# Layer norm on ScalarE, FP32 head products from Q in PSUM, and a reordered front in a fused attention and gated-MLP kernel

## The chip, the cores and the metric

The kernel runs on one core of one Trainium2 chip. A core has five engines that each work through their own instruction queue in order: TensorE (PE, matrix products into PSUM), VectorE (DVE), ScalarE (ACT), GpSimd (POOL) and SyncE (SP, here only issuing DMAs). They meet through semaphores. The metric is the device time of one execution in microseconds. The kernel before took 272.57 us as the median of three runs (272.36 to 272.59).

## The reference

The input `x` has 2048 rows of 640. Two branches are added to it, both in bf16:

```
xn = layernorm(x)                                # no gain, no bias
q, k, v = split(xn @ wqkv)                       # 32 heads of 20
logits[h, s, w] = q[h, s] . k[h, s - 2w] / sqrt(20)      # w = 0..7, -1e9 where s - 2w < 0
A = (sum_w softmax_w(logits) * v[h, s - 2w]) @ wo
B = ((x2 @ w_gate) * (x2 @ w_up)) @ w_down       # x2 = xn
out = x + A + B
```

Each row attends to eight rows: itself and every second row behind it. So the logits are no matrix product. They are elementwise products of Q with eight shifted copies of K, each summed over the 20 channels of a head.

## The kernel before

The work stands channels-first: 640 channels are five chunks of 128 partitions, and the 2048 rows are four blocks of 512, called `j` here. The weight columns of Q and K are picked with a stride of five, so that a head's 20 channels lie as four neighbouring partitions in each of the five chunks.

- **Front** (`front`, L513 to L570). For each of 16 tiles of 128 rows: two `bn_stats` and one `bn_aggr` on DVE (L522, L525), a square root on ACT (L528), then a reciprocal and the normalisation on DVE (L532, L533). Tiles 0 to 4 are transposed by TensorE (L552) and copied by DVE (L560); the others by a transposing DMA (L567). Ahead of the first tile TensorE runs 22 products of zeros, and three more after the first transpose (`warm`, L572).
- **Projections** (`proj_qk`, `proj_v`, products at L590). Q and K are evacuated from PSUM by ACT (L595) into `QT` and `KT`, V into `VST` and then to a scratch tensor in HBM. The first two row tiles need only the Q weights, in two loads; the K weights come in the next load.
- **Products and head sums** (`products`, L715; `logits`, L733). For block `j`, each of the five chunks and each half `r` of the eight window places, DVE multiplies Q, repeated four times, with four shifted views of K: one bf16 instruction of 128 x 2048. There are 40, in twelve buffers `PRD`. TensorE sums over the channels with a 0/1 matrix `G`: four products of 32 columns for each buffer, 160 in all, accumulated over the five chunks.
- **Softmax** (L762 to L786) on DVE, exponential on ACT (L777), once for blocks 0 and 1, once for 2 and 3.
- **Weighted V** (`unit`). For each of 20 units (block, chunk) DVE multiplies the weights, held in PSUM, with shifted V (L879, FP32 results in `PV`), GpSimd adds pairs of those (L884), and TensorE sums over partitions (L925). The V views `VX` lie where `QT` and `KT` were.
- **Gated MLP and output** (`gu`, L966; `dn`, L1024). Gate and up products fill PSUM banks; ACT copies the gate half to `HT` (L595), DVE multiplies the up half into it (L975). `dn` accumulates twelve products with `WD` and five with `WO`, DVE adds x (L1035), and a DMA stores the tile.

**What sets the order.** `Sched.run` (L220) is a planner that runs when the program is built. Every step is a `Task` with an engine, a priority and what it reads; each operation has a cost in microseconds (`occ`). The planner takes the task that can start first on its own clocks, and lower priority numbers among those close by. The result is one fixed order for each engine, which the chip then follows: an engine whose next instruction waits does nothing else. `lock` makes the planner keep DVE and GpSimd operations that carry it apart in time.

`gu(0)` may begin when all Q and K are projected, `gu(1)` when V is and all four head sums are issued (L942 to L951), since `HT` lies over `WQKV` and over some `PRD`. Four more lines matter:

```
WQKV = sb("WQKV", [128, 3, NCH, D], at=a_ra)      # L377: Q, K, V in this order
K.spawn(proj_group([(which, m, 1)], j * JB, JB, 12 + j, None))      # L658: blocks 2 and 3
yield Task("pe", go, r=[slots[-1][1][:]], prio=9.5, banks=2, slack=0.5)      # L754: head sums
yield Task("pe", go, r=[SV[u % NS][:] for u in us], prio=9.7, banks=len(us), slack=0.7)      # L939
```

Of the kernel before, what the change touches and what calls it, by code (L numbers as in the profile page):

```python
# [9 lines left out]
D = 640  # L10
# [330 lines left out]
def build_kernel(nc, A_x, A_wqkv, A_wo, B_x, B_w_gate, B_w_up, B_w_down, out):  # L341
# [58 lines left out]
    ATX = [ATX0, sb("ATX1", [128, 2, 2, JB])]  # L400
    PRD += [sb("PRD10", [128, 4, JB], at=place[0] - 4096), sb("PRD11", [128, 4, JB], at=place[0])]
    NPR = len(PRD)
    NXR = 3
    a_xr = place[0]
    XR = sb("XR", [128, NXR, D])
# [4 lines left out]
    MV = sb("MV", [128, NT, 16], FP32)  # L410
    SD = sb("SD", [128, NT, 16], FP32)
    DUM = sb("DUM", [128, 16], FP32)
    ZERO = sb("ZERO", [128, JB])
    EPSC = sb("EPSC", [128, 16], FP32)
    IDENT = sb("IDENT", [128, 128])
# [5 lines left out]
    def ht(j, m):  # L421
        return HX[m][:] if j % 3 == 2 else HT[:, j % 3, m, :]

    done = set()
    count = {}

# [6 lines left out]
    def have(*k):  # L433
        return lambda: k in done

    def num(n, *k):
        return lambda: count.get(k, 0) >= n
# [32 lines left out]
    wqkv_src = A_wqkv.rearrange("(c p) n -> p c n", p=128)  # L470

    def wqkv_load(g, lo=0, hi=NCH):
        dst = WQKV[:, g, lo:hi, :]
        dma(dst, wqkv_src[:, lo:hi, g * D:(g + 1) * D], w=[dst], name=f"ld_wqkv{g}_{lo}")

    def loads():
# [36 lines left out]
    def front(t):  # L513
        x, st = XST[:, xslot(t), :], STATS[:, t, 0:12]
        xs, mv = XNS[:, t % NXN, :], MV[:, t, 0:2]
        sd, rstd = SD[:, t, 0:1], SD[:, t, 1:2]
        p = 0.1 * t

        def stats():
            for i in range(2):  # L520
                o, a = st[:, 6 * i:6 * i + 6], x[:, i * DHALF:(i + 1) * DHALF]
                op("dve", (lambda o, a: lambda e: e.bn_stats(o, a))(o, a), r=[a], w=[("st", t, i)], name=f"bn{t}_{i}", occ=0.49)  # L522

        def aggr():
            op("dve", lambda e: e.bn_aggr(mv, st), r=[("st", t, 0), ("st", t, 1)], w=[("mv", t)], name=f"bnag{t}", occ=0.2)  # L525

        def sqrt():
            op("act", lambda e: e.activation(sd, mv[:, 1:2], ACT.Sqrt, bias=EPSC[:, 0:1]), r=[("mv", t), EPSC[:]],  # L528
               w=[("sd", t)], name=f"sd{t}", occ=0.25)

        def apply():
            op("dve", lambda e: e.reciprocal(rstd, sd), r=[("sd", t)], w=[("rstd", t)], name=f"rstd{t}", occ=0.16)  # L532
            op("dve", lambda e: e.tensor_scalar(xs, x, mv[:, 0:1], rstd, op0=ALU.subtract, op1=ALU.mult),  # L533
               r=[x, ("mv", t), ("rstd", t)], w=[xs], name=f"lnap{t}", occ=0.45)
            mark("apply", t)

        yield have("x", t)
        yield Task("dve", stats, r=[x], prio=p)
        yield Task("dve", aggr, r=[("st", t, 1)], prio=p)
        yield Task("act", sqrt, r=[("mv", t)], prio=p)  # L540
        if t >= NXN:
            yield have("xnt", t - NXN)
        yield Task("dve", apply, r=[("sd", t), x], w=[xs], prio=p)
        o = XNT[:, :, t * TS:(t + 1) * TS]
        if t < N_PE_T:
            hold = []

            def trans(b):
                tpv = PS[:, b, :].bitcast(BF16)[:, 0:NCH * 128].rearrange("p (c f) -> p c f", c=NCH)
                for c in range(NCH):  # L550
                    i, q = xs[:, c * 128:(c + 1) * 128], tpv[:, c, :]
                    op("pe", (lambda q, i: lambda e: e.transpose(q, i, IDENT[:]))(q, i), r=[i, IDENT[:]], w=[q],  # L552
                       name=f"tr{t}_{c}", occ=0.057, lat=0.2)
                hold.append((b, tpv))
                if t == 0:
                    warm(3)

            def copy():
                b, tpv = hold[0]
                X = op("dve", lambda e: e.tensor_copy(o, tpv), r=[tpv], w=[o], name=f"xntcp{t}", occ=0.49)  # L560
                K.free_bank(b, X)

            yield Task("pe", trans, r=[xs], prio=p, banks=1)
            yield Task("dve", copy, r=[PS[:, hold[0][0], :]], prio=p)
        else:
            def dmat():
                op("sp", lambda e: e.dma_start_transpose(o, xs), r=[xs], w=[o], dma=True, name=f"dtr{t}", nbytes=200e3, occ=1.25, extra=1.3)  # L567

            yield Task("sp", dmat, r=[xs], prio=1)
        mark("xnt", t)  # L570
# [5 lines left out]

    def wcols(which, c, m):
        if which == 2:
            return WQKV[:, which, c, m * 128:(m + 1) * 128]
        return WQKV[:, which, c, m:D:NCH]  # L580

    def mms(parts, b, name):
        order = [(p, c) for p in parts for c in range(NCH)]
# [58 lines left out]
    def proj_qk():  # L642
# [11 lines left out]
        for j in (2, 3):  # L654
            yield have("xnt", 4 * j + 3)
            for m in range(NCH):
                for which in (0, 1):
                    K.spawn(proj_group([(which, m, 1)], j * JB, JB, 12 + j, None))  # L658

    def proj_v(j, m):  # L660
        hold = []
# [11 lines left out]
            yield have("xnt", t)  # L673
        for t in range(NT) if j >= 2 else range(8, 12) if j else ():
            yield have("apply", t)
        yield Task("pe", go, r=[WQKV[:, 2, 4, 0:64], XNT[:, NCH - 1, j * JB:(j + 1) * JB]], prio=30 + j, banks=1)
        yield Task("act", ev, r=[PS[:, hold[0], :]], prio=6)

    def store_v(j):
# [6 lines left out]

        yield Task("sp", go, r=[VST[:, j]], prio=20)

    pairs = [(j, r) for j in range(NJ) for r in (1, 0)]
    QORD = list(range(4))  # L690

    def products():
        n = 0
        for j, r in pairs:
            if r == 1:
                slots = []
            for c in range(NCH):
                for which in (0, 1):
                    yield num(4, "qk", which, j, c)
                    if which == 1 and j > 0:  # L700
                        yield num(4, "qk", 1, j - 1, c)
                if n % NPR == NPR - 1:
                    yield have("xnt", NT - 1)
                if n >= NPR:
                    yield have("prd", n - NPR)
                s = PRD[n % NPR]
                base = KT[:, c, :]
                lo = PAD + j * JB - DIL * (3 + 4 * (1 - r))
                kv = bass.AP(base.tensor, base.offset + lo, [base.ap[0], [DIL, 4], [1, JB]])
                q = QT[:, j, c, :]  # L710
                qb = q.unsqueeze(1).to_broadcast([128, 4, JB])
                rk = KT[:, c, lo:lo + JB + 3 * DIL]

                def go(s=s, kv=kv, q=q, qb=qb, rk=rk, c=c):
                    op("dve", lambda e: e.tensor_tensor(s[:], qb, kv, ALU.mult), r=[q, rk], w=[s[:]],  # L715
                       name=f"prod{j}_{r}_{c}", occ=1.15, lock=True)

                yield Task("dve", go, r=[q, rk], w=[s[:]], prio=20 + j, lock=True)
                slots.append((n, s, r, c))
                n += 1  # L720
            if r == 0:
                K.spawn(logits(j, slots))

    def logits(j, slots):
        hold = []

        def go(*bs):
            for n, s, r, c in slots:
                b = bs[1 - r]
                for a in range(4):  # L730
                    o = PS[32 * a:32 * a + 32, b, :].rearrange("p (q s) -> p q s", q=4)
                    x = s[:, :, a * TS:(a + 1) * TS]
                    op("pe", (lambda o, x, a, c: lambda e: e.matmul(o, G[:], x, start=(c == 0), stop=(c == NCH - 1),  # L733
                                                                   tile_position=(0, 32 * a)))(o, x, a, c),
                       r=[G[:], x], w=[o], name=f"lg{j}_{r}_{c}_{a}", occ=0.054, lat=0.4, mode=1)
                mark("prd", n)
            hold.extend(bs)

        def dst(r):
# [11 lines left out]
                        m = LOG[0][0:32, 0, 4 * r + s, 0:DIL * w]  # L751
                        op("pool", (lambda m: lambda e: e.memset(m, NEG))(m), w=[m], name=f"mask{w}", occ=0.2)  # L752

        yield Task("pe", go, r=[slots[-1][1][:]], prio=9.5, banks=2, slack=0.5)  # L754
        bump("lg")
        for r in (1, 0):
            yield Task("act", lambda: ev(r), r=[PS[:, hold[1 - r], :]], w=[dst(r)], prio=2)
# [183 lines left out]

    def gu(j):  # L942
        if j == 0:
            for which in (0, 1):
                for m in range(NCH):
                    for jj in range(NJ):
                        yield num(4, "qk", which, jj, m)
        elif j == 1:
            for jj in range(NJ):
                yield num(NCH, "v", jj)  # L950
            yield num(NJ, "lg")  # L951
        elif j == 2:
            yield have("atx", 1)
        else:
            yield num(8, "dn", j - 3)
        if j:
            yield have("gu", j - 1)
        for m in range(NF):
            h = ht(j, m)
            hold = []  # L960

            def go(which, b):
# [90 lines left out]
                K.spawn(fin_thread())  # L1053

    N_PE_T = 5
    FIRST = 9
    GU_KEEP = 3

    x_load(0)
    x_load(1)  # L1060
    wqkv_load(0, 0, 3)
    wqkv_load(0, 3, NCH)
# [1 line left out]
    wqkv_load(1)  # L1064
    x_load(3)
    K.t["act"] = 2.1
    warm(22)

    def misc():
        yield have("xnt", NT - 1)  # L1070

        def sel():
            for q in range(4):
                a, b = SEL[32 * q:32 * q + 32, :], IDENT[32 * q:32 * q + 32, 32 * q:32 * q + 32]
                op("dve", (lambda a, b: lambda e: e.tensor_copy(a, b))(a, b), r=[b], w=[a], name=f"sel{q}", occ=0.1)

        yield Task("dve", sel, prio=19)
        yield Task("act", lambda: op("act", lambda e: e.activation(DUM[:, 0:1], EPSC[:, 0:1], ACT.Exp), r=[EPSC[:]], w=[DUM[:]],
                                     name="exp_preload", occ=1.3), prio=6)
# [56 lines left out]
```

## Time and profile before

The profiled execution took 272.77 us, of which 270.8 us are its span from the first to the last instruction.

| | |
|---|---|
| median of three runs | 272.57 us |
| profiled execution, its span | 272.77 us, 270.8 us |
| DVE busy | 224.9 us (83%), 286 instructions |
| ACT busy | 93.2 us (34%), 169 instructions |
| POOL busy | 96.5 us (36%), 57 instructions |
| granted TensorE clock | 1.000 |
| all DMA | 33.46 MB, mean 124 GB/s |

Times are in microseconds from the start of the span. A row of a timeline gives start, duration, engine, line, operation, what is written and read, and how often; in brackets the idle time before it and who ended it. A row of the chain gives start, duration and what held the end of the program back at that time. A row of the groups gives all instructions of one line and shape: total busy time, mean of one in ns, then idle time before them. "Busy" of one instruction overlaps its neighbour when they follow closely, so the pace of a row of equal instructions is its total divided by their number.

### The profile page before, as it was taken

How to read it: one execution, taken by the hardware profiler on the slowest of the kernel's cores; microseconds unless marked ns; L12 is line 12 of the kernel's file. 1: busy time of each engine (PE TensorE's matmuls, PEld its weight loads, DVE VectorE, ACT ScalarE, POOL GpSimd, SP SyncE). 2: the span in 40 equal slices, each digit the busy share in tenths (PEclk: the TensorE clock that was granted, in tenths of full speed). 3: DMA queues.
4: the chain of work that ended last, by engine and by line, in shares of the span. 5: the costliest groups of instructions: out<-in, count | busy, mean ns of one | idle time of the engine just before them, and what ended most of it. 6: DMA issues, size and time to landing. Idle time of an engine off the chain costs nothing.

```text
span 270.8 us, 4489 instructions
## 1 busy us (share of the span) xinstructions
PE 265.4 (98%) x1811; PEld 153.6 (57%) x1811; DVE 224.9 (83%) x286; ACT 93.2 (34%) x169; POOL 96.5 (36%) x57
## 2 busy tenths in 40 slices
PE   7899999999999999999999999999999999999995
PEld 5897965454444444444444577544676776444775
DVE  5777799999999989999999999889989998623221
ACT  2466676555753245222433400433201202242000
POOL 1000000000000004077756876677857996600000
PEclk9999999999999999999999999999999999999999
DMA  6965459702343999127723356633364531100101
GB/s 202 361 207 83 92 81 322 264 0 97 99 130 78 240 207 319 39 49 163 177 69 80 105 130 166 185 83 79 79 174 132 138 88 48 48 2 0 48 27 48
DMA packets 39571, 33.46 MB, mean 124 GB/s; under 512 B 15232, under 2 KB 38272, under 8 KB 39552
## 3 DMA queue, kind: packets, MB, share of 16 engines
q1 hardware_dynamic: 39408, 33.15, 45.7%
q8 instruction: 14, 0.23, 0.4%
q10 hardware_dynamic: 144, 0.04, 0.1%
q14 instruction: 5, 0.04, 0.1%
HBM read 25.07 MB, written 5.26 MB: 112 GB/s over the span
## 4 chain that ended last, share of the span: by engine, by line
PE 89%; DVE 5%; DMA 3%; issue 1%; SPq 1%; ACT 0%; DVEq 0%
PE PS L966 33%; PE PS L1024 27%; PE PS L590 23%; DMA WQKV<-in_A_wqkv_dram 3%; PE PS L733 3%; PE PS L925 2%; DVE SM L762 2%; DVE PV L879 1%; SPq L446 1%; DVE HT L975 1%; DVE RS L782 1%; DVE M L762 0%; DVE LOG L773 0%; ACT PS L864 0%; PE PS L552 0%
## 5 line engine op out<-in xcount | busy, mean ns | idle before, releaser
L884 POOL TENSOR_TENSOR SV<-PV 128x1024 bf16<-128x1024 f32 x40 | 94.8, 2380 | 86.9 <-DVE PV L879 86.7
L879 DVE TENSOR_TENSOR PV<-VX,PS 128x1024 f32<-128x1024 bf16 (+1 forms) x56 | 92.9, 1670 | 1.7 <-ACT PS L864 1.7
L590 PE MATMUL PS<-XNT,WQKV 128*128 128x512 bf16 (+2 forms) x480 | 66.7, 299 | 1.2 <-DVE XNT L560 1.0
L966 PE MATMUL PS<-XNT,WG 128*128 128x512 bf16 x240 | 59.7, 379 | 0.1
L966 PE MATMUL PS<-XNT,WU 128*128 128x512 bf16 x240 | 59.7, 379 | 0.0
L590 PEld LDWEIGHTS PS<-XNT,WQKV 128*128 128x128 bf16 x480 | 43.4, 113 | 24.0 <-DVE XNT L560 1.7
L715 DVE TENSOR_TENSOR PRD<-QT,KT 128x2048 bf16<-128x2048 bf16 x40 | 46.1, 1218 | 0.0
L1024 PE MATMUL PS<-WD,HT 128*128 128x320 bf16 (+1 forms) x300 | 43.2, 294 | 0.0
L966 PEld LDWEIGHTS PS<-XNT,WU 128*128 128x128 bf16 x240 | 23.2, 98 | 29.1 <-ACT HT L595 0.8
L966 PEld LDWEIGHTS PS<-XNT,WG 128*128 128x128 bf16 x240 | 23.3, 98 | 28.6 <-DVE HT L975 0.6
L595 ACT ACTIVATE HT<-PS 128x512 bf16<-128x512 f32 x36 | 21.5, 597 | 51.6 <-PE PS L966 51.6
L1024 PEld LDWEIGHTS PS<-WD,HT 128*128 128x128 bf16 x300 | 28.6, 98 | 11.6 <-issue 0.4
L975 DVE TENSOR_TENSOR HT<-HT,PS 128x512 bf16<-128x512 bf16 x36 | 23.9, 683 | 12.7 <-PE PS L966 12.7
L1035 DVE TENSOR_TENSOR FOUT<-PS,XR 128x320 bf16<-128x320 f32 (+1 forms) x33 | 15.8, 478 | 16.9 <-PE PS L1024 16.5
L1024 PE MATMUL PS<-WO,OT 128*128 128x320 bf16 (+1 forms) x165 | 27.1, 295 | 0.0
L934 ACT ACTIVATE OT<-PS 128x512 bf16<-128x512 f32 x20 | 10.5, 600 | 36.8 <-PE PS L925 36.8
L1024 PEld LDWEIGHTS PS<-WO,OT 128*128 128x128 bf16 x165 | 15.9, 98 | 5.9
L752 POOL MEMSET LOG<- 32x6 bf16 (+6 forms) x7 | 0.4, 95 | 51.5 <-ACT LOG L744 51.5
L595 ACT ACTIVATE QT<-PS 128x512 bf16<-128x512 f32 (+1 forms) x22 | 12.3, 558 | 9.6 <-PE PS L590 9.5
L522 DVE BATCH_NORM_STATS2 STATS<-XST 128x6 f32<-128x320 bf16 x32 | 13.9, 476 | 2.0 <-DMA XST<-in_A_x_dram 1.9
L595 ACT ACTIVATE KT<-PS 128x512 bf16<-128x512 f32 (+1 forms) x22 | 12.2, 556 | 8.1 <-PE PS L590 8.1
L595 ACT ACTIVATE VST<-PS 128x512 bf16<-128x512 f32 x20 | 11.7, 597 | 8.1 <-PE PS L590 8.1
(43 smaller groups left out, 128.3 us busy)
## 6 DMA issues: line engine op xcount, KB each, us to landing
VX<-v_scratch SPq DMA_DIRECT2D x80, 130.0 KB, 2.9
XST<-in_A_x_dram SPq DMA_DIRECT2D x16, 160.0 KB, 7.1
v_scratch<-VST SPq DMA_DIRECT2D x4, 640.0 KB, 4.1
XR<-in_A_x_dram SPq DMA_DIRECT2D x16, 160.0 KB, 2.9
out_dram<-FOUT SPq DMA_DIRECT2D x15, 160.0 KB, 2.4
WG<-in_B_w_gate_dram SPq DMA_DIRECT2D x1, 1920.0 KB, 8.4
WU<-in_B_w_up_dram SPq DMA_DIRECT2D x1, 1920.0 KB, 12.0
WD<-in_B_w_down_dram SPq DMA_DIRECT2D x1, 1920.0 KB, 8.9
```

Of the source, the lines that this page charges most:

```text
L522: op("dve", (lambda o, a: lambda e: e.bn_stats(o, a))(o, a), r=[a], w=[("st", t, i)], name=f"bn{t}_{i}", occ=0.49)
L590: op("pe", (lambda o, l, x, c, first: lambda e: e.matmul(o, l, x, start=first, stop=(c == NCH - 1)))(o, l, x, c, first), r=[l, x], w=[o], ...
L595: X = op("act", (lambda o, i: lambda e: e.activation(o, i, ACT.Copy))(o, i), r=[i], w=[o], name=name, occ=0.12 + n * 0.9e-3)
L715: op("dve", lambda e: e.tensor_tensor(s[:], qb, kv, ALU.mult), r=[q, rk], w=[s[:]], name=f"prod{j}_{r}_{c}", occ=1.15, lock=True)
L733: op("pe", (lambda o, x, a, c: lambda e: e.matmul(o, G[:], x, start=(c == 0), stop=(c == NCH - 1), tile_position=(0, 32 * a)))(o, x, a, c) ...
L879: op("dve", lambda e: e.tensor_tensor(p, vw, a, ALU.mult), r=[vv] + rk, w=[p], name=f"pv{u}_{x}_{r0}", occ=0.09 + 1.1 * nr)
L884: X = op("pool", lambda e: e.tensor_tensor(o, p[:, :, 0, :], p[:, :, 1, :], ALU.add), r=[p[:]], w=[o], name=f"pva{u}_{x}", occ=2.36, lock= ...
L934: X = op("act", (lambda o, b: lambda e: e.activation(o, PS[:, b, :], ACT.Copy))(o, b), r=[PS[:, b, :]], w=[o], name=f"oev{u}", occ=0.58)
L966: op("pe", (lambda l, x, c: lambda e: e.matmul(PS[:, b, :], l, x, start=(c == 0), stop=(c == NCH - 1)))(l, x, c), r=[l, x], w=[PS[:, b, :] ...
L975: X = op("dve", lambda e: e.tensor_tensor(h, h, PS[:, hold[1], :], ALU.mult), r=[h, PS[:, hold[1], :]], w=[h], name=f"h{m}_{j}", occ=0.65)
L1024: op("pe", (lambda l, x, i: lambda e: e.matmul(dst, l, x, start=(i == 0), stop=(i == n - 1)))(l, x, i), r=[l, x], w=[PS[:, b, :]], name=f" ...
L1035: X = op("dve", lambda e: e.tensor_tensor(o, PS[:, b, 0:wid], xr, ALU.add), r=[PS[:, b, :], xr], w=[o], name=f"fin{t}_{nb}", occ=0.15 + wi ...
```

## The change

Six things are changed together.

1. **Normalisation.** For tiles 6 to 15 the normalisation is one ACT instruction, `Identity(x * rstd + nmr)`, with both scalars read per partition. DVE makes `nmr = -mean * rstd` with one more small instruction. The reciprocal is a task of its own, the two `bn_stats` are separate tasks, and the square root gets a better priority.
2. **Block 3.** For chunks 0 to 3 Q is not evacuated. Its bank is kept, and DVE multiplies it, from PSUM, with two shifted views of K at a time into an FP32 buffer of 128 x 1024 (`PRD32`, which lies over `PRD`): 16 instructions in place of 8. GpSimd adds the results of chunks 0 and 1, and of 2 and 3, into bf16 buffers: 8 additions. The head sums of block 3 take 6 buffers and 24 products instead of 10 and 40.
3. **Buffers.** `PRD` slots come from a free list instead of a ring.
4. **Weights.** In SBUF the order is now K, V, Q. `gu(0)` waits for K and V, `gu(1)` for Q, and the head-sum condition moves to its seventh group.
5. **Start.** 18 products of zeros instead of 22; the first statistics of tile 1 follow the ones of tile 0 at once.
6. **A small DMA** on ACT's queue reads 128 pieces of 64 bytes of `wqkv` into an unused buffer.

The core of the diff:

```diff
@@ front @@
-    sd, rstd = SD[:, t, 0:1], SD[:, t, 1:2]
+    sd, rstd, nmr = SD[:, t, 0:1], SD[:, t, 1:2], SD[:, t, 2:3]
...
+    def recip():
+        op("dve", lambda e: e.reciprocal(rstd, sd), r=[("sd", t)], w=[("rstd", t)], name=f"rstd{t}", occ=0.16)
+        if t >= N_DVE_A:
+            op("dve", lambda e: e.tensor_scalar(nmr, mv[:, 0:1], rstd, -1.0, op0=ALU.mult, op1=ALU.mult),
+               r=[("mv", t), ("rstd", t)], w=[("nmr", t)], name=f"nmr{t}", occ=0.13)
...
+            op("act", lambda e: e.activation(xs, x, ACT.Identity, bias=nmr, scale=rstd),
+               r=[x, ("nmr", t), ("rstd", t)], w=[xs], name=f"lnap{t}", occ=0.75)
...
-    yield Task("dve", stats, r=[x], prio=p)
+    if t == 1:
+        yield have("sd", 0)
+    for i in range(2):
+        yield Task("dve", lambda: stats(i), r=[x], prio=-1 if t == 1 and i == 0 else p)
     yield Task("dve", aggr, r=[("st", t, 1)], prio=p)
-    yield Task("act", sqrt, r=[("mv", t)], prio=p)
+    yield Task("act", sqrt, r=[("mv", t)], prio=p - 1)
+    yield Task("dve", recip, r=[("sd", t)], prio=p)
@@ proj_qk @@
-                    K.spawn(proj_group([(which, m, 1)], j * JB, JB, 12 + j, None))
+                    if which or j not in WIDE or m == NCH - 1:
+                        K.spawn(proj_group([(which, m, 1)], j * JB, JB, 12 + j, None))
@@ products @@
+def q_bank(j, c, hold):
...
+    yield Task("pe", go, r=[wcols(0, NCH - 1, c), XNT[:, NCH - 1, j * JB:(j + 1) * JB]], prio=8, banks=1, keep=1)
+def wide(j, slots):
+    for c0 in (0, 2):
...
+        for r in (1, 0):
...
+            for q0 in (0, 2):
+                for c in (c0, c0 + 1):
...
+                    def go(o=o, qb=qb, kv=kv, q=q, rk=rk):
+                        X = op("dve", lambda e: e.tensor_tensor(o[:], qb, kv, ALU.mult), r=[q, rk], w=[o[:]],
+                               name=f"prow{j}_{r}_{c}_{q0}", occ=1.17)
...
+                K.spawn(pair_add(j, s, n, q0, f, parts))
+def pair_add(j, s, n, q0, f, parts):
...
+        op("pool", lambda e: e.tensor_tensor(o, a[:], b[:], ALU.add), r=[a[:], b[:]], w=[o], name=f"padd{j}_{n}_{q0}",
+           occ=2.36, lock=True)
@@ gu @@
     if j == 0:
...
+                yield num(4, "qk", 1, jj, m)
         for jj in range(NJ):
             yield num(NCH, "v", jj)
-        yield num(NJ, "lg")
+    elif j == 1:
...
+                yield num(4, "qk", 0, jj, m)
...
+        if j == 1 and m == 6:
+            yield num(NJ, "lg")
@@ start @@
+N_DVE_A = 6
 x_load(0)
+tch = A_wqkv.rearrange("(p r) n -> p r n", r=NCH)[:, 0, 0:32]
+stores.append(dma(TCH[:], tch, w=[TCH[:]], name="touch", eng="act"))
 x_load(1)
...
-warm(22)
+warm(18)
```

In the fixed orders that the planner now writes, TensorE has the same 160, 120 and 200 projection products of 128, 256 and 512 columns. Five of 256 columns (the last chunk of Q for tiles 0 and 1) stand ahead of the first K group instead of behind it. The first head sums stand 20 products of 512 columns earlier. The head sums of block 3 stand behind 125 products from those of block 2 on, instead of 55: twelve gate and up pairs are done by then. At the end, the sums of the last two units stand behind all of `gu(3)`, directly ahead of `dn(3)`.

## The prediction

> **What bounds the kernel now.** I read the busy shares first, then the chain that ended last, then TensorE's rows at the start, then the groups by shape.
>
> ```profile
> PE 265.4 (98%) x1811; PEld 153.6 (57%) x1811; DVE 224.9 (83%) x286; ACT 93.2 (34%) x169; POOL 96.5 (36%) x57
> ```
>
> TensorE is busy for 98% of the span. The chain shows the same, and where its work stands:
>
> ```profile
> 3.24 7.55 DMA WQKV<-in_A_wqkv_dram
> ...
> 10.84 3.55 PE PS L590 x60
> 14.38 0.28 PE PS L552 x5
> 14.66 0.55 PE PS L590 x5
> ...
> 16.84 34.21 PE PS L590 x245
> 51.05 2.27 PE PS L733 x40
> ...
> 249.51 18.53 PE PS L1024 x153
> ```
>
> The end is set by the K weights, which land at 10.79, and from then on by TensorE's own work. The table of stretches has TensorE busy for 5.96 of 6.00 us from 10.84, all of 16.84 to 96.0, and all but some 0.1 us up to 230. So only two things shorten this kernel: less TensorE work behind 10.84, or more of it ahead of that point. Anything done on DVE, ACT or POOL pays only by not making TensorE wait.
>
> The start, from TensorE's timeline:
>
> ```profile
> 1.26 4.59 PE L574 MATMUL PS<-ZERO 128*128 128x256 bf16 x22 [1.26 <-DVE EPSC L449]
> 9.03 1.31 PE L590 MATMUL PS<-XNT,WQKV 128*128 128x128 bf16 x20 [0.72 <-DVE XNT L560]
> 10.18 0.44 PE L552 MATMUL PS<-IDENT,XNS 128*128 128x128 bf16 x5
> 10.84 3.55 PE L590 MATMUL PS<-XNT,WQKV 128*128 128x128 bf16 x60 [0.22 <-DMA WQKV<-in_A_wqkv_dram]
> ```
>
> There is a hole of 0.72 us before Q of tile 1 and one of 0.22 before K: about one microsecond in which Q work could stand. The durations that I use, from the groups by shape:
>
> ```profile
> L879 DVE TENSOR_TENSOR PV<-VX,PS 128x1024 f32<-128x1024 bf16 x32 | 38.2, 1213 | 1.7 <-ACT PS L864 1.7
> L715 DVE TENSOR_TENSOR PRD<-QT,KT 128x2048 bf16<-128x2048 bf16 x40 | 46.1, 1218 | 0.0
> L884 POOL TENSOR_TENSOR SV<-PV 128x1024 bf16<-128x1024 f32 x40 | 94.8, 2380 | 86.9 <-DVE PV L879 86.7
> L528 ACT ACTIVATE SD<-MV,EPSC 128x1 f32<-128x1 f32 x16 | 4.6, 290 | 5.3 <-DVE MV L525 5.2
> L1078 ACT ACTIVATE DUM<-EPSC 128x1 f32<-128x1 f32 x1 | 0.2, 203 | 0.0
> ```
>
> **Less TensorE work.** The head sums of block 3 fall from 40 products to 24. Forty take 2.27 us on the chain, 0.057 each; 16 of them are 0.91 us, and they stand where TensorE is never idle. All other counts of products are equal in both orders. That is the first term: **-0.91**.
>
> **More ahead of the K weights.** Five products of 256 columns (last chunk of Q, tiles 0 and 1) move from behind the first K group to before it; the chain gives them 0.55 us at 14.66. Is there room? Four zero products fewer (22 took 4.43 us up to the transpose at 5.69, 0.20 each) end the fill at about 4.9 to 5.1. Statistics of tile 1 go into the gap of the first square root, so the normalisation of tile 0 ends near 5.4 instead of 5.26 and the transpose starts there, not at 5.69. Q of tile 0 then starts near 6.45 (was 6.72). For tile 1, its copy is queued behind one `bn_stats` instead of two (0.44 us less than 8.50, with the wait for the transpose about 8.25), and Q runs from 8.75 to 10.06. The moved five end at 10.61, the transpose of tile 2 (0.28) at 10.89. K can start at 10.89 against 10.84. Net **-0.50**. I let the K weights land as before: the small new DMA has 128 pieces, and the nearest row, queue q10, spent 0.1% of sixteen engines' span on 144 packets, 0.27 us for each DMA engine. So it costs 0 to 0.3, where the hole leaves about 0.05; it could also make the weights earlier, but then DVE holds TensorE at 10.89 all the same. Its issue on ACT (about 0.4 us, as SP's) lies ahead of the table load, and the first square root starts only at 4.28.
>
> The Trainium skill speaks against cutting the fill. TensorE: Matmul & The Clock Gate, Part 1, says that TensorE starts at half clock and needs some 3.4 us of sustained work, measured in a free-running window, to be let up. The granted clock column shows 1.00 throughout, but the rows agree with the page: the zero products took 0.20 us each, while 256 columns later take 0.11. The change happened before 5.69, near 5.4 if the first twenty took 0.213. With 18 the fill would end at 5.1 and leave a gap of 0.3 us right there. By the rows the clock rises as before and the term stays -0.50; by the rule a missed window would leave it low until about 8.8, everything up to Q of tile 1 starts 0.5 us later, and the term is 0. I take the rows, as nine tenths of the window stay busy, and keep +0.5 for the range.
>
> **ACT in the front.** The row for 512 elements (0.597) and for 256 (0.383) give 0.84 ns an element, so 0.71 us for 640 without scalar operands. The skill, ScalarE: Activation LUTs, What ACT_TABLE_LOAD costs, says that each per-partition operand adds about 93 ns; the rows say 87 (290 with one, 203 without). With two, 0.89 to 0.92; I take 0.92, of which the next instruction overlaps 0.09. The loop from one tile to the next: normalisation 0.83, square root 0.29, reciprocal and new scalar 0.16 each with 0.04 hand-over: 1.56 to 1.6 us. ACT's queue agrees, 0.83 + 0.2 + one evacuation at 0.5 back to back. With 0.71 it would be 1.4. Before, tile 6 was normalised at 20.38 and tile 15 at 38.07, 1.97 us a tile. So with 1.58 tile 15's scalars stand at 20.4 + 9 x 1.58 = 34.6.
>
> Who waits for that? Evacuations are queued behind the normalisations: four or five are late at once near 33 us, of eight banks. Then the products. The first is done by 34.9, tile 15's two scalars (0.4), a second product, four small copies (0.7), eight more products at 1.14 (26.21 us for 23): the tenth ends near **46.2**. The first head sums stand 20 products of 0.216 earlier, and TensorE reaches them at 51.05 - 4.32 - 0.50 = **46.2**. Before, DVE was ready 1.6 us ahead. This is a tie; I charge **+0.1**, and keep 0 to 1.0.
>
> **Block 3.** Sixteen FP32 products are near the PV row (same shape, a PSUM operand, FP32 out): 1.21 busy, 1.14 at pace, 18.2 us, for eight at 9.1. They run between 76.7 and 101 with ten multiplications of the up half (0.60 each), while TensorE has gate and up work until about 107; the last two bf16 products end near 105.6, so 1.5 us spare. Eight GpSimd additions, 2.36 each, lie beside that. PV products beside additions show no slowing. Two-input SBUF work does: `SM` at 105.63 took 3.18 us for two where the earlier pair took 1.15, beside an addition that took 3.26. That price, 2.0 once, stands in both kernels; a second time, at the last bf16 products, it would overdraw the 1.5 by 0.5.
>
> **Weighted V comes later.** Softmax of blocks 2 and 3 ends near 122.3 instead of 111.8. Counting DVE's order at pace (2.2 for a PV of 2048, 0.60, 0.41 for an output), unit 2 ends near 138.2, its addition near 140.7; TensorE arrives near 141.4. Before, the addition ended at 130.2 and TensorE came at 130.97: the same 0.7 to 0.8 us. Unit 19 ends near 243.4 with the idle time of before (7 us), its addition at 245.8, TensorE at 247.4. No wait, so **0**; bounds 0 to 0.8. It cannot gain, as TensorE was not waiting there. Four evacuations fewer, the free list and the weights' order likewise: nothing waited for them. The price if that cover goes is in the rivals.
>
> **Sum.** -0.91 - 0.50 + 0.10 = -1.31 us. The profiled execution would take 272.77 - 1.31 = 271.46; it lies 0.20 above the median, so the median goes to 272.57 - 1.31 = **271.3**.
>
> **Rivals.**
> - *The gain is partly eaten at the start* (the clock comes up late, K lands late, or the first head sums wait 0.3 to 1.0): for it, the tie at 46.2 and a hole of 0.05; against it, that the tie comes from DVE's measured pace. Gain 0.56 to 1.0, **271.8**.
> - *The start gives nothing and DVE is late somewhere behind it*, at unit 2 or at block 3, whose slacks are 0.7 and 1.5: gain 0.91 less some 0.8, **272.5**, no difference.
> - *ScalarE becomes the bound of the front, and it gets slower.* Place: the loop from tile 6 to 15. Every 0.1 us more on a tile makes the tenth product 0.9 us later, and TensorE stands before the first head sums with nothing else in its order. Above 1.58 + 1.4/9 = 1.74 us a tile the whole gain is gone; if each tile also waits for a full evacuation (0.3 more, 1.88), the wait is 2.7 us and the time **273.9**. For it: ACT stands in this loop twice and its queue has an evacuation for each tile. Against it: these evacuations are ready before their turn by my times.
>
> **How the numbers follow.** A difference of 0.2%, 0.55 us, is about what a measurement of this kernel can tell from none. The forecast has 0.56, the eaten gain 0.25, no difference 0.10, slower 0.09. Faster 0.81, the same 0.10, slower 0.09. The range: no wait and K at 10.84 give 271.1, with DVE or the weights better than I count some 0.3 less; the upper end takes in the eaten gain and the edge of no difference: 270.8 to 272.3.
>
> **What would show it.** 144 head sums on TensorE, busy about 264.5; the 60 K products start near 10.9 with 45 Q products ahead of them; no idle before the first head sums near 46.2 (a wait for DVE `PRD` there is the second or fourth case, and its length says which); the normalisation near 0.92 on ACT and 1.6 us from tile to tile; FP32 products near 1.21; DVE busy near 232, POOL 115, ACT 100; head sums of block 3 near 107. I am wrong if TensorE shows waits of over 0.3 us before any head sum, or if its idle time ahead of 10.9 is not filled.

## The result, and the profile after

The changed kernel took 271.47 us, the median of six runs (271.11 to 272.07), beside 272.47 us for the kernel before on the same chip (six runs, 272.08 to 272.59). The ratio is 0.9967, with a 95% interval of 0.9954 to 0.998: about 0.9 us faster. The profiled execution also took 271.47 us, with a span of 269.7 us. By the chain, TensorE's last product ended at 267.01 instead of 268.04, which is 1.03 us earlier. The granted clock of the run was 1.000.

The busy shares on the page of the changed kernel:

```profile
PE 264.3 (98%) x1791; PEld 152.7 (57%) x1791; DVE 231.9 (86%) x294; ACT 98.4 (36%) x175; POOL 115.2 (43%) x65
```

TensorE has 20 instructions fewer: 16 head sums and four products of zeros. DVE has 7 us more and GpSimd 19 us more, and TensorE is still the engine that sets the time. Here is its chain, with start, duration and what held the end back:

```profile
10.99 3.35 PE PS L610 x60
...
16.80 29.35 PE PS L610 x220
46.15 2.27 PE PS L816 x40
...
107.27 1.41 PE PS L816 x24
108.68 13.05 PE PS L1052 x60
121.73 0.08 issue
121.81 0.02 DVEq L319
121.83 0.79 issue
122.62 0.69 DVE HT L1061
123.32 0.04 issue
123.36 18.52 PE PS L1052 x85
141.88 0.76 PE PS L1008 x12
...
248.37 18.64 PE PS L1110 x153
```

Three things are to be seen. The first head sums (x40) follow their predecessor without any pause. The head sums of block 3 are 24 products in 1.41 us. And at 121.7 the chain leaves TensorE for 1.6 us: it goes over issue time (in which an engine waited for nothing that the profile shows) to a multiplication of DVE (L1061, the up half into `HT`), and only then on with gate and up products at 123.36. The kernel before had such a place too, among the lines of its chain that the prediction left out: from 96.0 to 112.5 its chain runs over the softmax on DVE, and it comes back to TensorE here:

```profile
111.78 0.69 DVE HT L975
...
112.52 18.52 PE PS L966 x85
```

TensorE's timeline at the start. The last column, in brackets, is the idle time ahead and who ended it:

```profile
1.26 4.02 PE L594 MATMUL PS<-ZERO 128*128 128x256 bf16 x18 [1.26 <-DVE EPSC L453]
5.38 0.71 PE L569 MATMUL PS<-IDENT,XNS 128*128 128x128 bf16 x5
...
8.86 1.86 PE L610 MATMUL PS<-XNT,WQKV 128*128 128x128 bf16 x25 [0.58 <-DVE XNT L578]
...
10.83 3.51 PE L610 MATMUL PS<-XNT,WQKV 128*128 128x128 bf16 x60
```

Ahead of the K group (x60) stand 25 Q products in a row where 20 stood before. The hole ahead of K is gone, and that ahead of Q of tile 1 is 0.58 instead of 0.72. Three groups by shape (line, total, mean ns, idle time before):

```profile
L780 DVE TENSOR_TENSOR PRF<-PS,KT 128x1024 f32<-128x1024 f32 x16 | 19.0, 1218 | 0.3 <-PE PS L816 0.2
...
L546 ACT ACTIVATE XNS<-XST,SD 128x640 bf16<-128x640 bf16 x10 | 9.2, 920 | 0.9 <-DVE SD L538 0.9
L816 PE MATMUL PS<-PRD,G 128*32 128x512 bf16 x144 | 8.5, 380 | 0.0
```

### Where the time went

One number makes the runs comparable. The start of the K group shifts from run to run by some tenths (it stands at 10.6 to 11.4 in the traces below). What follows it does not: the stretch from the start of the K group to TensorE's last product repeats to 0.01 us in kernels that are equal behind that point. The start is read from the timeline, the end from the chain. The chain can't be used for the start: where a group follows another without a wait, the chain begins it at the end of the one before, here 0.16 us late (10.99 where the timeline has 10.83), and where TensorE waited, at its own start. In this table, "hole" is what TensorE loses behind the softmax of blocks 2 and 3: the start of the first late group of five gate or up products, less the time it was due, 1.08 us after the group before it began. (The idle time in a bracket is 0.16 less, as the profile lets each group end 1.24 us after its start.)

| kernel | K starts | first head sums | end of TensorE | K to end | hole |
|---|---|---|---|---|---|
| before | 10.84 | 51.05 | 268.04 | 257.20 | 0.30 |
| after | 10.83 | 46.15 | 267.01 | 256.18 | 0.71 |
| e1 | 10.87 | 46.19 | 269.40 | 258.53 | 2.18 |
| e2 | 11.29 | 52.00 | 274.30 | 263.01 | 0.70 |
| e3 | 10.82 | 46.68 | 267.53 | 256.71 | 0.70 |
| e4 | 11.16 | 46.49 | 266.63 | 255.47 | none |
| e5 | 10.70 | 47.12 | 267.96 | 257.26 | 0.70 |
| e6 | 10.93 | 51.64 | 267.54 | 256.61 | 0.29 |
| e7 | 10.90 | 46.25 | 267.27 | 256.37 | none |
| e8 | 10.92 | 46.24 | 267.10 | 256.18 | 0.70 |
| e9 | 11.36 | 46.68 | 266.82 | 255.46 | none |
| e10 | 10.63 | 45.95 | 266.09 | 255.46 | none |
| e11 | 11.06 | 48.54 | 270.40 | 259.34 | 0.70 |
| e12 | 10.91 | 51.12 | 267.81 | 256.90 | none |

The hole in the kernel before, from the timelines of TensorE and of DVE over 100 to 118 us:

```profile
111.14 1.24 PE L966 MATMUL PS<-XNT,WU 128*128 128x512 bf16 x5
112.52 1.25 PE L966 MATMUL PS<-XNT,WG 128*128 128x512 bf16 x5
```

```profile
110.64 1.22 DVE L786 TENSOR_TENSOR LOG<-LOG,RS 128x2048 bf16<-128x2048 bf16 x1
111.78 3.07 DVE L975 TENSOR_TENSOR HT<-HT,PS 128x512 bf16<-128x512 bf16 x5
```

Groups of five follow each other by 1.08 us, so the one at 112.52 was due at 112.22. The multiplications that empty its PSUM banks were queued behind the last step of the softmax and began at 111.78. In the changed kernel the same thing is larger (timeline of all engines, 104 to 127 us):

```profile
115.22 1.22 DVE L845 TENSOR_TENSOR SM<-LOG 128x1024 f32<-128x1024 bf16 x1
115.38 3.27 POOL L967 TENSOR_TENSOR SV<-PV 128x1024 bf16<-128x1024 f32 x1 [11.69 <-DVE PV L962]
...
116.47 3.19 DVE L845 TENSOR_TENSOR SM<-SM 128x512 f32<-128x512 f32 x2
...
119.69 1.75 DVE L865 RECIPROCAL RS<-SM 128x256 bf16<-128x256 f32 x1
...
121.48 1.22 DVE L869 TENSOR_TENSOR LOG<-LOG,RS 128x2048 bf16<-128x2048 bf16 x1
...
122.62 2.47 DVE L1061 TENSOR_TENSOR HT<-HT,PS 128x512 bf16<-128x512 bf16 x4
...
123.36 1.25 PE L1052 MATMUL PS<-XNT,WU 128*128 128x512 bf16 x5 [0.55 <-DVE HT L1061]
```

From 115.2 to 122.6 DVE works through the softmax in one piece. Four multiplications of the up half wait behind it, each holding a bank. TensorE runs out of free banks; the group due at 122.65 starts at 123.36. That is 0.71 us lost where 0.30 was lost before. DVE's rows of this stretch are the same in both kernels, 10.84 us later now (111.78 and 122.62), while the group of TensorE was due only 10.43 us later (112.22 and 122.65): TensorE comes 0.41 us earlier to the same wait.

So the 1.03 us come out of the trace in three terms. The first head sums were due at 51.05 - 20 x 0.216 = 46.73 if nothing had changed but the order of the projections, and started at 46.15: **-0.58** for the start. Forty head sums take 2.27 us and 24 take 1.41: **-0.86**. The hole: 0.71 - 0.30 = **+0.41**. The sum is -1.03.

### The profile page after: what moved, and what is told of

It is laid out like the page before. It is cut to its first block, busy times and chain, and to the rows that moved or that the text cites. A ratio compares the mean times of both kernels' runs of the same rounds, so it can differ in the third digit from the quotient of the medians.

```text
span 269.7 us, 4474 instructions
## 1 busy us (share of the span) xinstructions
PE 264.3 (98%) x1791; PEld 152.7 (57%) x1791; DVE 231.9 (86%) x294; ACT 98.4 (36%) x175; POOL 115.2 (43%) x65
## 4 chain that ended last, share of the span: by engine, by line
PE 96%; DVE 2%; DMA 1%; issue 0%; DVEq 0%
PE PS L1052 38%; PE PS L1110 28%; PE PS L610 24%; PE PS L816 3%; PE PS L1008 2%; DMA XST<-in_A_x_dram 1%; PE PS L569 1%; DVE STATS L525 0%; DVE XNT L578 0%; DVE HT L1061 0%; DVE XNS L543 0%; DVE FOUT L1121 0%; DVE MV L528 0%; DVE SD L536 0%; DVEq L319 0%
## 5 line engine op out<-in xcount | busy, mean ns | idle before, releaser
L738 DVE TENSOR_TENSOR PRD<-QT,KT 128x2048 bf16<-128x2048 bf16 x32 | 36.8, 1218 | 0.0
L794 POOL TENSOR_TENSOR PRD<-PRF,PRF 128x1024 bf16<-128x1024 f32 x8 | 18.8, 2357 | 35.5 <-DVE PRF L780 35.5
L1061 DVE TENSOR_TENSOR HT<-HT,PS 128x512 bf16<-128x512 bf16 x36 | 24.1, 682 | 6.8 <-PE PS L1052 5.6
L780 DVE TENSOR_TENSOR PRF<-PS,KT 128x1024 f32<-128x1024 f32 x16 | 19.0, 1218 | 0.3 <-PE PS L816 0.2
L525 DVE BATCH_NORM_STATS2 STATS<-XST 128x6 f32<-128x320 bf16 x32 | 14.7, 469 | 2.0 <-DMA XST<-in_A_x_dram 2.0
L947 ACT ACTIVATE PS<-ATX 128x512 f32<-128x512 bf16 x8 | 4.8, 598 | 27.4 <-DVE PV L962 27.4
```

The source lines that it names most:

```text
L525: op("dve", lambda e: e.bn_stats(o, a), r=[a], w=[("st", t, i)], name=f"bn{t}_{i}", occ=0.49)
L780: X = op("dve", lambda e: e.tensor_tensor(o[:], qb, kv, ALU.mult), r=[q, rk], w=[o[:]], name=f"prow{j}_{r}_{c}_{q0}", occ=1.17)
L794: op("pool", lambda e: e.tensor_tensor(o, a[:], b[:], ALU.add), r=[a[:], b[:]], w=[o], name=f"padd{j}_{n}_{q0}", occ=2.36, lock=True)
L1061: X = op("dve", lambda e: e.tensor_tensor(h, h, PS[:, hold[1], :], ALU.mult), r=[h, PS[:, hold[1], :]], w=[h], name=f"h{m}_{j}", occ=0.65)
```

## The experiments

My theory after the result: start and head sums are worth what they should be, and the difference is lost in the hole, because DVE's order puts the up multiplications behind the softmax. The rivals: the start is worth nothing; ScalarE is at its limit; the parts can be had singly. Times are medians; each ratio is to the kernel before on the same chip.

### e1: without the FP32 products

```diff
-    WIDE = (3,)
+    WIDE = ()
```

> The changed kernel with block 3 as before (WIDE empty: Q of block 3 is evacuated, ten bf16 products, 40 head sums); normalisation on ScalarE and the new start stay. Theory (the gain is TensorE's own work: 0.91 us of head sums, about 0.5 us moved ahead of K, less 0.4 us more of a wait for PSUM banks behind the second softmax): 0.91 comes back, of the wait 0.4 goes, so about 0.5 us slower than the changed kernel, 272.0. Rival (the normalisation on ScalarE is what pays, by relieving VectorE): no difference, 271.5.

Measured: 273.46 us (273.09 to 274.43), ratio 1.0042, interval 1.0026 to 1.0059. Slower than the kernel before, so both expectations missed. TensorE's timeline and DVE's, around 108 us:

```profile
109.56 1.25 PE L1052 MATMUL PS<-XNT,WG 128*128 128x512 bf16 x5 [2.01 <-DVE HT L1061]
```

```profile
108.83 3.07 DVE L1061 TENSOR_TENSOR HT<-HT,PS 128x512 bf16<-128x512 bf16 x5
```

The hole is 2.18 us (idle 2.01). With DVE less loaded, the softmax of blocks 2 and 3 begins earlier (96.45), and five multiplications pile up behind it. Beside the kernel before, the start is worth -0.59 here (as in e6, from K to the end) and the hole +1.88, together +1.29; "K to end" is 1.33 longer. So the hole depends on where the planner puts the softmax among the multiplications. It made e1 useless as a price of the head sums; e7 is the repair.

### e2: the normalisation on DVE

```diff
-    N_DVE_A = 6
+    N_DVE_A = NT
```

> The changed kernel with all 16 normalisations on VectorE again (N_DVE_A = 16); block 3 and the start stay. Theory: VectorE is later by about 3.5 us in the front, the planner puts gate and up groups or projections ahead of the first head sums instead, and TensorE does the same work without waiting: 271.5, within 0.2 us of the changed kernel. Rival (the normalisation is what pays): back to the kernel before, 272.5.

Measured: 278.52 us (278.02 to 278.79), ratio 1.0223 (1.0209 to 1.0238): both missed by six us. TensorE's timeline at 162 us, and its stretches of 2 us (busy times of the five engines, then the granted clock, then the share and rate of the DMAs):

```profile
165.99 0.39 PE L1008 MATMUL PS<-SV,SEL 128*32 128x512 bf16 x2 [2.83 <-POOL SV L967]
168.30 0.61 PE L1008 MATMUL PS<-SV,SEL 128*32 128x512 bf16 x2 [1.92 <-POOL SV L967]
168.84 3.11 PE L1110 MATMUL PS<-WD,HT 128*128 128x320 bf16 x12
...
172.47 1.79 PE L1110 MATMUL PS<-WD,HT 128*128 128x320 bf16 x12
```

```profile
167.00:169.00 2.00, 0.70 (x3) 0.23 (x4) 2.00 (x2) 0.04 (x1) 2.00 (x2) 0.78 0.75 186
169.00:171.00 2.00, 2.00 (x9) 1.10 (x8) 2.00 (x2) 0.55 (x1) 2.00 (x2) 0.50 0.15 29
```

TensorE waits 2.83 and 1.92 us for GpSimd's additions before the second sums over partitions (L1008). The reason lies 100 us earlier: with the slow loop of the front and the 9 us of extra FP32 work, DVE is late by more than TensorE can bridge. Up to the first `dn`, TensorE may fill such waits with gate and up products, and all 360 were used; the kernel before had used 310 by then, so 50 products, 10.8 us, were its reserve. Then the wait costs a second time: the clock column falls to 0.50, and twelve products take 3.11 us instead of 1.79. The 4.75 us of waits and about 1.5 us of clock are most of the 6.8 us by which "K to end" exceeds that of the changed kernel; the rest I did not follow.

So the ScalarE normalisation gives TensorE nothing directly. It pays for the FP32 products. Without these it makes no difference: with the hole set aside, "K to end" is 256.32 with the normalisation on DVE (e6, 256.61 less 0.29) and 256.37 with it on ScalarE (e7).

### e3: the old start

```diff
-        if t == 1:
-            yield have("sd", 0)
-        for i in range(2):
-            yield Task("dve", lambda: stats(i), r=[x], prio=-1 if t == 1 and i == 0 else p)
+        yield Task("dve", lambda: (stats(0), stats(1)), r=[x], prio=p)
...
-    stores.append(dma(TCH[:], tch, w=[TCH[:]], name="touch", eng="act"))
...
-    warm(18)
+    warm(22)
```

> The changed kernel with the start as before: 22 zero products, both statistics of a tile together, no small DMA; so the five products of Q stand behind the first K group again. Theory: the K group starts near 10.84, TensorE ends 0.4 to 0.6 us later, 272.0. Rival (the start gives nothing, all of the gain is block 3): 271.5.

Measured: 271.79 us (271.16 to 272.42), ratio 0.9975 (0.9963 to 0.9986). That is 0.3 us above the changed kernel by the medians; by the trace the first head sums stand at 46.68 instead of 46.15, and TensorE ends 0.52 us later. K starts at the same time, but five Q products stand behind it again. The start is worth 0.5 us by the trace; the times agree in sign, and their intervals overlap.

### e4 and e9: the up multiplications before the softmax

```diff
-                yield Task("dve", mul, r=[h, PS[:, hold[1], :]], prio=15)
+                yield Task("dve", mul, r=[h, PS[:, hold[1], :]], prio=9)
```

Only DVE's order changes; those of TensorE and ScalarE stay.

> The changed kernel with the multiplication of the up half ahead of the softmax steps in VectorE's order (priority 9 instead of 15); TensorE's and ScalarE's orders are the same. Theory: the hole of 0.55 us on TensorE at 122.8 (no free PSUM bank, since four multiplications stand behind the softmax) closes: 0.5 to 0.7 us faster than the changed kernel, 270.9. Rival (weighted V is as late, so the wait is moved to the sums behind it): no difference, 271.5, with a wait before the first sums near 141.8.

Measured: 270.91 us (270.77 to 271.08), ratio 0.9947 (0.9935 to 0.9959). The chain, where the hole was:

```profile
107.60 1.41 PE PS L816 x24
109.01 32.48 PE PS L1052 x150
141.49 0.76 PE PS L1008 x12
```

150 products follow one another without a pause. The timelines of GpSimd (one row) and of DVE show how:

```profile
115.80 2.35 POOL L967 TENSOR_TENSOR SV<-PV 128x1024 bf16<-128x1024 f32 x1 [11.77 <-DVE PV L962]
115.97 3.26 DVE L845 TENSOR_TENSOR SM<-LOG 128x1024 f32<-128x1024 bf16 x1 [0.25 <-ACT LOG L860]
119.15 1.27 DVE L1061 TENSOR_TENSOR HT<-HT,PS 128x512 bf16<-128x512 bf16 x2
120.35 1.14 DVE L845 TENSOR_TENSOR SM<-SM 128x512 f32<-128x512 f32 x2
...
123.19 1.22 DVE L1061 TENSOR_TENSOR HT<-HT,PS 128x512 bf16<-128x512 bf16 x2
```

The multiplications now stand between the steps of the softmax. "K to end" falls from 256.18 to 255.47, by 0.71: the whole hole. DVE's work is the same in both, so its order alone made the hole. e9 is the same kernel again, run beside e10 on one chip:

> The changed kernel with the multiplication of the up half ahead of the softmax steps, once more, beside the next kernel. Theory: 0.5 to 0.7 us faster than the changed kernel, about 1.5 us faster than the kernel before. Rival: the first result was a lucky chip, less than 1.2 us.

Measured: 270.86 us (270.67 to 271.23), ratio 0.9934 (0.9919 to 0.9949), K to end 255.46.

### e5: is ScalarE at its limit in the front?

A spare ScalarE copy of 128 elements follows each of the ten normalisations.

```diff
+    SPARE = sb("SPARE", [128, 128])
...
+                op("act", lambda e: e.activation(SPARE[:], ZERO[:, 0:128], ACT.Copy), r=[ZERO[:]], w=[SPARE[:]], name="spare", occ=0.0)
```

> The changed kernel with a spare copy of 128 elements on ScalarE behind each of its ten normalisations, which the planner counts at nothing; all orders else are the same. Theory (the first head sums are a tie, so the front's loop is the bound from there on): the copy is near 0.18 us at pace, nine of them make the tenth product 1.6 us later, TensorE waits 1.4 to 1.6 us before the first head sums, 273.0. Rival (there is slack, because VectorE sets the pace of a tile and ScalarE hides): no difference, 271.5.

Measured: 272.32 us (271.92 to 272.77, 16 runs), ratio 0.9992 (0.9984 to 1.0): between the expectations. The copy takes 0.293 us and lengthens the loop from 1.585 to 1.785 us a tile. ScalarE's timeline, then those of TensorE and of DVE:

```profile
29.22 0.92 ACT L547 ACTIVATE XNS<-XST,SD 128x640 bf16<-128x640 bf16 x1
30.05 0.29 ACT L549 ACTIVATE SPARE<-ZERO 128x128 bf16<-128x128 bf16 x1
...
31.01 0.92 ACT L547 ACTIVATE XNS<-XST,SD 128x640 bf16<-128x640 bf16 x1
```

```profile
38.29 8.83 PE L612 MATMUL PS<-XNT,WQKV 128*128 128x512 bf16 x40 [0.60 <-ACT KT L617]
47.05 2.34 PE L818 MATMUL PS<-PRD,G 128*32 128x512 bf16 x40
```

```profile
38.38 13.71 DVE L740 TENSOR_TENSOR PRD<-QT,KT 128x2048 bf16<-128x2048 bf16 x12
```

ScalarE now works back to back. TensorE loses about 1 us, but not where my rival had put it: it waits for ScalarE to empty PSUM banks (0.60 of it at 38.29), and the first head sums at 47.05 wait for nobody. DVE's tenth product then ended at 38.38 + 8 x 1.142 = 47.5, half a microsecond after the group of head sums had begun. So a head sum waits for its own buffer only: the tenth is needed some 2 us after the first. This removes the "tie" of my sum. The first evacuation behind the last normalisation starts at 37.66 instead of 35.97, which is 1.8 us later counted from the start of K. That cost TensorE 1.10 us (first head sums 36.42 behind the start of K instead of 35.32), so ScalarE had some 0.7 us of slack in this loop.

### e6: the new start alone

```diff
-    WIDE = (3,)
+    WIDE = ()
...
-    N_DVE_A = 6
+    N_DVE_A = NT
```

> The kernel before with the new start alone: normalisation on VectorE and block 3 in bf16 with 40 head sums, K V Q order of the weights and the new conditions of gate and up stay. Theory: only the five moved products of Q pay, 0.5 us against the kernel before, 271.9. Rival (the new start needs the rest of the change): no difference from before, 272.4.

Measured: 272.38 us (271.89 to 274.2, 21 runs), ratio 0.9996 (0.9985 to 1.0006). Inconclusive: the trace has TensorE end 0.50 us before the kernel before (K to end 0.59 less, K 0.09 later), the times allow -0.4 to +0.2 us.

### e7: the price of the head sums

Without the FP32 products, but with the up multiplications ahead, so that the hole of e1 can't disturb.

```diff
-    WIDE = (3,)
+    WIDE = ()
...
-                yield Task("dve", mul, r=[h, PS[:, hold[1], :]], prio=15)
+                yield Task("dve", mul, r=[h, PS[:, hold[1], :]], prio=9)
```

> Block 3 in bf16 with 40 head sums as in the run without FP32 products, and the multiplication of the up half ahead of the softmax steps. Theory (that run was slow by the wait of 2.0 us for PSUM banks at 109.6, not by block 3 itself): the wait goes, and what is left against the changed kernel with the multiplication first (270.9) is the 16 head sums, 0.9 us: 271.8. Rival (without FP32 products some other cost stays, such as V views that land late): 273 or more.

Measured: 271.90 us (271.36 to 272.42), ratio 0.9974 (0.9962 to 0.9987). Against e4, which ran on another chip, it is 1.0 us by the medians and 0.7 by the two ratios; by "K to end" it is 256.37 - 255.47 = 0.90. The 16 head sums are worth 0.9 us, as the rows said.

### e8: 22 products of zeros in the changed kernel

```diff
-    warm(18)
+    warm(22)
```

> The changed kernel with 22 zero products at the start instead of 18. In the changed kernel the five transposes of tile 0 took 0.73 us instead of 0.28, so its clock came up later. Theory (cutting the fill gained nothing, since the slow transposes ate what the earlier start gave): Q of tile 0 starts near 6.7 again, K near 11.0, no difference, 271.5. Rival (the cut fill pays): 0.3 us slower, K near 11.3.

Measured: 271.54 us (271.32 to 271.69), ratio 0.996 (0.9947 to 0.9973), K to end 256.18. The time is as forecast, but not for the reason given. Here the clock came up early (22 products took 3.99 us), and Q of tile 0 started at 6.70 because TensorE waited 0.50 us for the Q weights. So e8 doesn't show what the shorter fill is worth; no run shows a gain or a cost. (Read in one view, the timeline, tile 0's transposes took 0.71 us in the changed kernel and 0.44 in the kernel before.)

### e10: e4 without the small DMA

```diff
-                yield Task("dve", mul, r=[h, PS[:, hold[1], :]], prio=15)
+                yield Task("dve", mul, r=[h, PS[:, hold[1], :]], prio=9)
...
-    stores.append(dma(TCH[:], tch, w=[TCH[:]], name="touch", eng="act"))
```

> As the last, without the small DMA on ScalarE's queue. Theory: the small DMA neither costs nor gives anything that can be measured, since K weights are not waited for: within 0.2 us of the last. Rival (it delays the Q weights, which land at 6.7 to 6.85 in some traces where TensorE waits 0.5 us for them): 0.3 to 0.5 us faster than the last, and Q of tile 0 starts near 6.4.

Measured: 270.51 us (270.2 to 270.74), ratio 0.9919 (0.9904 to 0.9934): the fastest version, 2.1 us below the kernel before and 0.35 below e9 beside it. Q of tile 0 on TensorE's timeline, in e9 and then in e10:

```profile
7.15 1.37 PE L610 MATMUL PS<-XNT,WQKV 128*128 128x128 bf16 x20 [1.05 <-DMA WQKV<-in_A_wqkv_dram]
```

```profile
6.42 1.37 PE L610 MATMUL PS<-XNT,WQKV 128*128 128x128 bf16 x20 [0.30 <-DVE XNT L578]
```

In e9 the Q weights arrive late, and everything behind them is 0.73 us later; "K to end" is the same, 255.46 in both. In e2, e4, e8 and e11 TensorE also waits for these weights, until 6.70 to 6.98; in the trace of the changed kernel it does not: the delay comes and goes with the run. The first Q weights landed at 5.86 to 6.28 in the four traces without the small DMA, and at 5.80 to 7.01 in the ten with it. What is shown is a difference of the two kernels in time, by six runs of each whose ranges just touch, and that in e9 the weights were what came late; how 128 small pieces on another queue delay them is not.

### e11: five tiles more on DVE

```diff
-    N_DVE_A = 6
+    N_DVE_A = 11
```

> The changed kernel with tiles 6 to 10 normalised on VectorE too (N_DVE_A = 11, five on ScalarE). Theory: with block 3 in FP32 all 360 gate and up products that may run before the first output block are used up when the second sums come, so VectorE's time is the bound there, with 0.8 us to spare; five tiles at 0.39 us more make VectorE 2.0 us later, TensorE waits 1.2 us before the second sums, 272.7. Rival (VectorE is no bound until much later, and the run with all tiles on VectorE was slow by its order alone): 271.5.

Measured: 274.57 us (274.23 to 277.39), ratio 1.0091 (1.0057 to 1.0125). The direction of the theory is right, its size is not. TensorE's timeline:

```profile
163.62 0.39 PE L1008 MATMUL PS<-SV,SEL 128*32 128x512 bf16 x2 [0.68 <-POOL SV L967]
165.93 0.39 PE L1008 MATMUL PS<-SV,SEL 128*32 128x512 bf16 x2 [1.92 <-POOL SV L967]
```

The first wait shrinks from 2.83 to 0.68 with half of the tiles on ScalarE, as the reserve theory wants. The second stays at 1.92: two units stand close together there, and GpSimd needs 2.36 us for each addition, so the last one is late whenever DVE is. I had not counted that. "K to end" is 3.16 us longer than in the changed kernel; the two waits are 2.60 of it, the rest is open.

### e12: the kernel before, with the up multiplications first

```diff
-                yield Task("dve", mul, r=[h, PS[:, hold[1], :]], prio=15)
+                yield Task("dve", mul, r=[h, PS[:, hold[1], :]], prio=9)
```

> The kernel before with the multiplication of the up half ahead of the softmax steps. Theory: the wait for PSUM banks behind the second softmax was in the kernel before too, 0.3 us at 112.2, and goes: 0.3 us faster than the kernel before. Rival (it came with the change only): no difference.

Measured: 272.34 us (271.71 to 273.1, 22 runs), ratio 0.9986 (0.9976 to 0.9995), K to end 0.30 less. The small hole of the kernel before was worth its 0.3 us, and the order that closes it helps more in the changed kernel (0.71) than here.

## Why the prediction was right, and where it was not

The forecast of 271.3 us stands beside 271.47 measured; its two main terms hold, and two smaller steps were wrong in opposite directions. That the numbers lie so close is in part luck: the kernel before took 272.47 beside it where the forecast started from 272.57, so the gain was 1.00 us by the medians, and 1.03 in the trace, where 1.31 was forecast.

- **Head sums, -0.91.** Measured -0.86 in the chain (2.27 to 1.41 us), and 0.9 by e7 against e4. Right.
- **Start, -0.50.** Measured -0.58 in the chain, and 0.52 in e3 by the end of TensorE. The five products moved, as planned (0.55), and K starts at 10.83 where it started at 10.84. I had said 10.89, from two errors that nearly cancel: Q of tile 1 came at 8.86 and not at 8.75, and I had added the 1.31 us of its row in full, although the next row begins 1.15 us after it (9.03 and 10.18 in the kernel before). e6 has -0.59 from K to the end.
- **The fill and the clock.** The Trainium skill's page TensorE: Matmul & The Clock Gate, Part 1, describes a free-running activity window, so that the same kernel warms up at different times. The traces agree: 18 products of zeros took 4.02 us in the changed kernel and in e10, 3.78 in e9 and 3.55 in e11; 22 took 4.59 before, 4.88 in e3 and 3.99 in e8. In the changed kernel the rise came after the first transposes, which took 0.71 instead of 0.44 us. So both sides of my weighing happen, with the same fill. The late case costs far less than the 0.5 that I kept for it: Q of tile 1 started at 8.86 where I had 8.75. A clock that stays low until 8.8 occurred in no run: where a trace records the rise of the granted clock, it stands between 3.92 us (e12, 22 products) and 6.94 (e6, 18).
- **The tie at 46.2, +0.10.** Both times were right: TensorE came at 46.15, and the tenth product ended at 36.89 + 8 x 1.142 = 46.0. The step failed in its premise that all ten must be there when the group begins. e5 showed the group running with the tenth still half a microsecond away. The charge is 0. By the rows the tenth buffer is needed 36 products of 0.054 us behind the first, so the slack was about 2 us.
- **"No wait, so 0" behind block 3.** This is the step that failed. I had moved the softmax of blocks 2 and 3 to 122.3 (measured 122.6) and asked only who needs its results. Unit 2 came as I said (its addition ended at 141.05, TensorE came at 141.88, a slack of 0.8). What I left out is what is queued behind the softmax on DVE: the up multiplications, which free PSUM banks. The hole cost +0.41 net. It already stood in the trace of before, with 0.30. There I had called TensorE busy for "all but some 0.1 us", since the busy time counts 0.16 of such a hole as work, and had written that the end is set "from then on by TensorE's own work", although the chain leaves TensorE from 96.0 to 112.5. e4 and e9 remove the hole.
- **The rival with ScalarE as the bound.** The normalisation took 920 ns, as 0.92 said (0.71 and two operands of 0.087 to 0.093 sum to 0.88 to 0.90; that the rounding up was exact is luck), and a tile 1.585 us. The last tile took 2.05, so tile 15 was normalised at 35.14 and not at 34.6. The rival's direction is right (e5), its place is not: late evacuations stop TensorE at the PSUM banks, before any head sum does.
- **Block 3.** FP32 products 1218 ns against 1.21, head sums at 107.27 against 107, GpSimd additions 2357 ns against 2.36. Right.

Net of the terms: -0.86 - 0.58 + 0.41 = -1.03 where I had -0.91 - 0.50 + 0.10 = -1.31. Open stay the time of e6, and why the small DMA delays the Q weights only in some runs.

## What to carry to other kernels

Before an operation is moved or made longer on an in-order engine, list what is queued behind it that gives back a shared resource: here it was not the softmax's result that was missed but the PSUM banks behind it, and a change of one priority returned 0.7 us. An engine off the critical path pays when its relief covers new work elsewhere: normalisation on ScalarE and FP32 products together with the start gain 1 us; without the former the kernel is 7 us slower, without the latter it loses 0.9 us of head sums, and 1.5 more where the order leaves a larger hole (e1). Measure from a fixed point behind the noisy start, and read that point in the same view for every run; from there, equal kernels agreed to 0.01 us, where their times spread over 0.5.

## What the runs showed of the hardware that I had not expected

- **A wait of TensorE can cost twice.** In e2, after waits of 2.83 and 1.92 us with two short products in between, the granted clock was 0.78 in the stretch from 167 to 169, 0.50 in that from 169 to 171 and 1.00 again from 173 on; it cost about 1.5 us on top of the 4.75. In e11, waits of 0.68 and 1.92 us left the clock at 1.00 and the next twelve products at 1.80 us. Where between the two cases the clock falls, no run shows.
- **In these rows DVE and GpSimd exclude each other by whole instructions.** In the changed kernel GpSimd's addition, 2.36 us elsewhere, takes 3.27 at 115.38, while DVE's two-input FP32 sum from SBUF (1.22 from 115.22) runs; then DVE's next pair, 1.15 elsewhere, takes 3.19 and ends 1.0 us after the addition. In e4 the addition starts first, at 115.80, and takes 2.35; now DVE's instruction takes 3.26 instead of 1.22 and ends 1.1 us after it. One goes, the other waits until it is done. The Trainium skill, Trainium Architecture — The Big Picture, What this means for kernel authors, calls it "an exclusive lock (not a bandwidth split)"; these rows agree. FP32 products with one operand in PSUM showed none of it (1218 ns beside the additions).
